# Three seven-product units for one batch of a sigmoid-attention and ReGLU kernel: batch 1's last four f chunks as a third unit, two chunks of batch 0 moved into batch 2

## The chip, the cores and the metric

The kernel runs on one core of a Trainium2 chip. The metric is device time of one execution in microseconds (us), median over runs. A core has engines that run side by side, each its own instruction stream in program order: TensorE (PE: matrix products, with its weight loads shown as PEld), VectorE (DVE: arithmetic element by element), ScalarE (ACT: functions such as sigmoid, copies), GpSimd (POOL: here above all the engine that issues loads) and SyncE (SP: here stores and transposing transfers). PE writes its results into eight banks of PSUM; DVE and ACT read them from there, and a bank can be written again only when its readers are through. Engines wait for one another by semaphores.

## The reference

```python
def _attn_ref(q, k, v):                      # 8 batches, 12 heads, 448 tokens, 64 per head
    scale = 1.0 / np.sqrt(q.shape[-1])
    scores = scale * np.matmul(q, k.transpose(0, 1, 3, 2)) - np.log(S)
    attn = 1.0 / (1.0 + np.exp(-scores))
    return np.matmul(attn, v)

def _moe_ref(x, w_gate, w_val, w_out):       # 3584 x 768, 768 x 1536 (twice), 1536 x 768
    gate = np.maximum(x @ w_gate, 0.0)
    val = x @ w_val
    return gate * val @ w_out
```

The attention's output, with heads side by side, is the x of the second part. Input and output are float32; the kernel multiplies in float16 and sums in float32.

## The kernel before

**Attention.** Heads go in groups of four, so a batch has three groups (g = 0, 1, 2). Tokens of a group go in seven chunks of 64 keys. `qk_unit` makes one chunk's scores: four matmuls into two banks (L239), then two sigmoids on ACT (L187), one for each bank. `pv_group` multiplies a whole group's probabilities with v: 28 matmuls into two banks (L257) and two evacuations on DVE (L184) into `xT`, the transposed x that the second part reads. The 21 chunks of a batch are cut into *bursts* (`cuts`), with the pv of one group within a burst (`pv_at`; that of a batch's last group lies in the next batch's first burst). Between two bursts PE does other work while ACT catches up on sigmoids.

**Keys and queries** must be transposed. For batch 0 and batch 1 PE does it (`pe_transposes`, L204, and a copy by DVE); from batch 2 on `dma_transposes(b, g)` does: two DVE copies into a buffer `rel` (L222; two such buffers) and a transposing transfer on SP's queue (L226) from `rel` to `qkT`.

**The second part.** f counts 12 chunks of 128 of the 1536 hidden columns. Simple form, `gv`: six matmuls for the gate and six for the value of one f chunk (L322), a relu (ACT, L334, or DVE, L336) and a multiplication on DVE (L343), result in `hT`. Batch 0's are computed in halves of 256 and 192 tokens (`push_first`), as filling in batch 1 (`ffn_mix`; `mix` says how many after which burst). All later work is done with seven products in place of eight, on sums of operand blocks:

- `gv_split` ("s", L688): one batch, four f chunks. Seven products of 12 matmuls on half of the tokens (L708), six copies out of PSUM (two of them on DVE, L719, four on ACT), six additions (L723) and four multiplications with relu (L729) on DVE. It needs sums of weight blocks (`early_sum_steps`, three sums and `gate_sums` for two chunks each) and of token blocks (`split_sums`).
- `gv_pair` ("w"): the same for two batches and two f chunks.
- `down_pair` ("y", L448): the last matmul for two tiles of 128 tokens, seven products of six matmuls (L385), on sums of `wo` (`weight_sums(0)` to `(3)`, 128x2304 each, L376) and of `hT` (`token_sum_steps`, 128x768 each). Where a burst lies amid it (`amid`, "inner burst"), the order of the seven products depends on whether the unit is in `SUMS_LATE`: if so, y11's product comes second, in a bank `a` taken at the beginning, and five products lie ahead of the inner burst; otherwise four, and y11's bank is taken behind it.

**Order.** Nothing is scheduled by a planner: each engine's order is the order in which this program writes its instructions. `for b in range(1, B)` goes through the batches; for each burst it writes the burst, then a filler with `jobs` (work of other engines written amid the filler, by `beside`) and `ahead` (written ahead of it). Batch 1's fillers are halves of batch 0; batch 2's come from `push_group(0)`: chunk 8 of batch 1, unit s0 (chunks 0 to 3), chunk 9, unit s4, chunks 10 and 11. Batch 3's fillers are the down units y of batches 0 and 1. PSUM banks are taken in turn from a ring (`free`); `later` changes the ring's order.

**Loads** are issued by POOL; a load waits until the one eight places before it has landed. `hold` puts a tiny POOL copy in the queue that waits for a transpose to land, so that later loads do not run beside it. Batch 1's k and q lie in the pool `early`, which also holds twelve `PT` buffers whose space the weight sums of s0 and s4 take over; `open_late` closes `early` and opens `late` with the sums of `wo` (`T`), `odd` and token-block sums (`X`).

Of the kernel before, what the change touches and what calls it, by code (L numbers as in the profile page):

```python
# [18 lines left out]
def kernel(  # L19
# [10 lines left out]
    nc = tc.nc  # L30
# [28 lines left out]
    gsbp = ctx.enter_context(tc.tile_pool(name="gsbp", bufs=6))  # L59
    first_sbuf = ExitStack()  # L60
# [34 lines left out]
    def tiles_of(b):  # L95
        if b not in in_tiles:
            pool = early if b == 1 else inp
            in_tiles[b] = tuple(
                p.tile([P, NPAIR, NCH * D], FP16, tag=t, name=t)
                for p, t in ((pool, "k16"), (pool, "q16"), (vinp, "v16"))  # L100
            )
        return in_tiles[b]
# [54 lines left out]
    load_gv(6, 9)  # L157
    load_v(1)
    load(1, 2, 3, "kq")
    load_gv(9, 12)  # L160
# [57 lines left out]
    def dma_transposes(b, g):  # L218
# [9 lines left out]
        )  # L228

# [136 lines left out]
    def open_late():  # L366
# [5 lines left out]
        late["X"] = pool.tile([P, 3, HD, S], FP16, tag="X", name="X")  # L372
        late["sums"] = ctx.enter_context(tc.tile_pool(name="sums", bufs=2))

# [28 lines left out]
    SUMS_LATE = {(1, 0), (1, 1), (2, 0), (2, 1), (3, NPP)}  # L403
# [152 lines left out]
    def early_sum_steps(j, f):  # L556
        views = []
        for i in range(3 * j, 3 * j + 3):
            t = early.tile([P, 2, 512], FP16, tag=f"PT{i}", name="S")
            flat = t[:].rearrange("p a y -> p (a y)")[:, 0 : HD * 2 * P]  # L560
            views.append(flat.rearrange("p (x y) -> p x y", y=2 * P))
# [15 lines left out]
    def batch_blocks(g, ks):  # L577
        x1, x2 = xT_tiles[2 * g], xT_tiles[2 * g + 1]
        lo, hi = slice(*ks), slice(HD + ks[0], HD + ks[1])
        return [late["X"][:, i, lo] for i in range(3)] + [x1[:, lo], x1[:, hi], x2[:, lo], x2[:, hi]]  # L580
# [13 lines left out]
    def gv_pair(g, f, beside, first_copy):  # L594
        x1, x2 = xT_tiles[2 * g], xT_tiles[2 * g + 1]
        T1, T2, T4 = (late["X"][:, i] for i in range(3))
# [77 lines left out]
    def split_sums(b):  # L674
        tile_ = xTp.tile([P, NPAIR, S], FP16, tag="xT", name="X2")
# [165 lines left out]
    push_first(1, range(0, 4))  # L841
    for f0 in range(4, 12, 2):
        for half in range(2):
            for f in range(f0, f0 + 2):
                push_first(half, (f,), (half, f) not in ((0, 9), (1, 8)))
# [10 lines left out]
    def hold(b, g):  # L856
        nc.gpsimd.tensor_copy(gate[0:1, :], qkT_tiles[(b, g)][0:1, 0, 0:2])
# [4 lines left out]

    def late_loads():
        dma_transposes(2, 2)
        hold(2, 1)
        load_v(2)
        load(3, 0, NG, "kq")
        load_o()

# [5 lines left out]
    def push_group(g):  # L875
        tail = [("y", g, p) for p in range(NPP)]
        if g == 0:
            work.extend([("u", 1, 8), ("s", 1, 0), ("u", 1, 9), ("s", 1, 4), ("u", 1, 10), ("u", 1, 11)])
# [45 lines left out]
    for b in range(1, B):  # L924
        if b == 1:
            cuts, pv_at = (0, 3, 6, 9, 13, 17, 21), {3: (0, 2), 5: (1, 2)}
        else:
            cuts, pv_at = (0, 4, 7, 11, 14, 18, 21), {0: (-1, 2), 2: (0, 2), 4: (1, 2)}
# [8 lines left out]
        if b == 1:  # L937
            mix = (4, 3, 3, 3, 3, 4)
            hooks = {
                1: [(3, lambda: both(1, 1))],  # L940
                3: [(3, lambda: both(1, 2))],
                4: [(2, lambda: dma_transposes(2, 0)), (0, lambda: dma_transposes(2, 1))],
                5: [(4, late_loads)],
            }
            steps = itertools.chain.from_iterable(early_sum_steps(j, 2 * j) for j in range(4))
            given = ((0, 0, 1, 1, 1), (0, 1, 1, 1), (0, 1, 1, 1), (0, 1, 1, 0), (2, 0, 0, 0), (0, 1, 1, 1, 0))
# [16 lines left out]
        for m in range(count):  # L963
# [92 lines left out]
```

## Time and profile before

| | us |
|---|---|
| median of 3 runs | 388.73 (388.58 to 389.12) |
| the profiled execution, its own time | 389.02 |
| its span, first to last instruction | 387.2 |
| PE busy | 381.0 |
| DVE busy | 304.5 |
| ACT busy | 227.3 |
| POOL busy | 49.9 |
| batch 1, span 29.0 to 61.3: DVE busy / ACT busy | 21.67 / 24.43 of 32.30 |
| batch 2, span 61.3 to 95.8: DVE busy / ACT busy | 26.39 / 23.72 of 34.50 |
| mean granted clock of PE | 0.998 |

Times in a trace count from the span's start. A line of the timeline gives start, length, engine, source line, operation, result and operands, shapes and how many instructions were merged into it; in brackets idle time ahead of it and what ended it. Durations overlap at their ends, so what one more instruction costs is read from start to start. The waits list says for each engine, line and cause how long it waited in all, how often, and the longest. Windows give span, then busy time and instruction count for PE, PEld, DVE, ACT and POOL, then granted clock, DMA share and GB/s.

### The profile page before, as it was taken

What the parts mean: (1) busy time and instruction counts of PE and PEld (TensorE: products, weight loads), DVE (VectorE), ACT (ScalarE), POOL (GpSimd) and SP (SyncE); (2) the same over time, 40 slices, a digit from 0 to 9 for tenths busy, and PEclk for the clock granted to TensorE, in tenths of its full rate; (3) what the DMA queues carried; (4) which work ended last, traced back from release to release, by engine and by line L of the source; (5) the groups of instructions that cost most, each with busy time, mean ns of one, the idle gap of its engine ahead of it and who ended that gap; (6) DMA issues with size and microseconds to landing.
All of it is one profiled execution on the core that took longest, in us unless ns stands there. A gap on an engine that the chain in (4) does not pass through costs nothing.

```text
span 387.2 us, 8977 instructions
## 1 busy us (share of the span) xinstructions
PE 381.0 (98%) x3570; PEld 223.2 (58%) x3570; DVE 304.5 (79%) x609; ACT 227.3 (59%) x480; POOL 49.9 (13%) x73
## 2 busy tenths in 40 slices
PE   8999999999999999999999999999999999999995
PEld 6678776885555545555555554545455555555563
DVE  3455667769868999999868789999978788999563
ACT  5967887567777645555777764545477344333321
POOL 9543306100400003000300300000000000000000
PEclk9999999999999999999999999999999999999999
DMA  9999999999969303952599893222012220000335
GB/s 169 199 199 204 204 194 163 208 208 130 182 150 193 81 2 40 184 90 47 44 228 224 164 231 60 48 50 50 0 38 72 71 69 0 2 0 0 83 88 159
DMA packets 67421, 43.81 MB, mean 113 GB/s; under 512 B 35634, under 2 KB 64050, under 8 KB 67378
## 3 DMA queue, kind: packets, MB, share of 16 engines
q0 software_dynamic: 28960, 23.24, 39.3%
q1 hardware_dynamic: 37634, 19.24, 24.4%
q10 hardware_dynamic: 784, 0.75, 0.6%
q8 instruction: 28, 0.46, 0.5%
q14 instruction: 15, 0.12, 0.1%
HBM read 47.19 MB, written 11.01 MB: 150 GB/s over the span
## 4 chain that ended last, share of the span: by engine, by line
PE 97%; ACT 2%; DVE 0%; issue 0%
PE u L385 35%; PE g L385 16%; PE y L385 12%; PE qk_ps L239 10%; PE pv_ps L257 8%; PE g_ps L322 5%; PE v_ps L322 5%; PE u L708 2%; PE g L708 2%; ACT PT L187 2%; PE warm_ps L175 1%; PE trt L204 1%; ACT ysb L446 0%; DVE ysb L540 0%; DVE zeros L130 0%
## 5 line engine op out<-in xcount | busy, mean ns | idle before, releaser
L187 ACT ACTIVATE PT<-qk_ps 128x448 f16<-128x448 f32 (+3 forms) x318 | 150.9, 584 | 79.7 <-PE qk_ps L239 79.5
L385 PEld LDWEIGHTS <-S 128*128 128x128 f16 x576 | 56.4, 98 | 45.9
L624 DVE TENSOR_TENSOR gsb<-g,gsb 128x448 f32<-128x448 f32 x72 | 42.8, 624 | 8.0 <-PE g L385 7.7
L239 PE MATMUL qk_ps<-qkT 64*64 64x448 f16 (+2 forms) x756 | 47.5, 337 | 1.0 <-ACT ysb L446 0.6
L385 PEld LDWEIGHTS <-hT 128*128 128x128 f16 x318 | 29.5, 98 | 24.0 <-issue 6.1
L257 PE MATMUL pv_ps<-PT,v 64*64 64x448 f16 (+2 forms) x756 | 36.6, 329 | 0.0
L464 DVE SCALAR_TENSOR_TENSOR ysb<-y,ysb 128x384 f32<-128x384 f32 x33 | 18.4, 556 | 21.3 <-PE y L385 14.3
L184 DVE TENSOR_SCALAR xT<-pv_ps 128x448 f16<-128x448 f32 (+2 forms) x53 | 27.8, 567 | 8.2 <-PE pv_ps L257 7.1
L385 PEld LDWEIGHTS <-wg 128*128 128x128 f16 x216 | 20.1, 98 | 21.8 <-issue 4.3
L385 PEld LDWEIGHTS <-wv 128*128 128x128 f16 x216 | 21.1, 98 | 19.7
L446 ACT ACTIVATE ysb<-u 128x384 f32<-128x384 f32 x28 | 13.8, 491 | 30.6 <-PE u L385 26.5
L239 PEld LDWEIGHTS <-qkT 64*64 64x64 f16 x756 | 17.7, 106 | 21.3 <-issue 14.2
L385 PE MATMUL u<-wo,hT 128*128 128x384 f16 x156 | 29.8, 327 | 0.0
L111 POOL DMA_DIRECT2D k<-in_k_dram x14 | 10.9, 776 | 142.0 <-DVE rel L222 136.3
L257 PEld LDWEIGHTS <-v 64*64 64x64 f16 x756 | 21.4, 107 | 11.1 <-issue 0.5
L385 PE MATMUL u<-xT,wg 128*128 128x448 f16 x108 | 23.5, 354 | 0.0
L385 PE MATMUL u<-X,S 128*128 128x448 f16 x108 | 23.4, 352 | 0.0
L385 PE MATMUL g<-xT,wg 128*128 128x448 f16 x108 | 23.4, 352 | 0.0
L385 PE MATMUL u<-X,wv 128*128 128x448 f16 x108 | 23.4, 352 | 0.0
L385 PE MATMUL g<-X,S 128*128 128x448 f16 x108 | 23.4, 352 | 0.0
L385 PE MATMUL g<-xT,S 128*128 128x448 f16 x108 | 23.4, 352 | 0.0
L385 PE MATMUL u<-xT,wv 128*128 128x448 f16 x108 | 23.4, 352 | 0.0
(98 smaller groups left out, 563.1 us busy)
## 6 DMA issues: line engine op xcount, KB each, us to landing
out_dram<-ysb SPq DMA_DIRECT2D x50, 192.0 KB, 3.9
v<-in_v_dram POOLq DMA_DIRECT2D x8, 336.0 KB, 15.3
v<-in_v_dram POOLq DMA_DIRECT2D x16, 168.0 KB, 15.2
k<-in_k_dram POOLq DMA_DIRECT2D x4, 672.0 KB, 12.0
q<-in_q_dram POOLq DMA_DIRECT2D x4, 672.0 KB, 15.0
wo<-in_moe_w_out_dram POOLq DMA_DIRECT2D x2, 1152.0 KB, 19.2
k<-in_k_dram POOLq DMA_DIRECT2D x9, 224.0 KB, 12.1
q<-in_q_dram POOLq DMA_DIRECT2D x7, 224.0 KB, 12.4
```

Source lines behind the costliest of these rows:

```text
L111: nc.gpsimd.dma_start(t16[:, xs, cs], rows_of(src, b)[:, xs, cs])
L175: nc.tensor.matmul(ps[:, 0:n], zeros[:, 0:P], zeros[:, 0:n], start=True, stop=True)
L184: nc.vector.tensor_scalar(out=xT, in0=src, scalar1=XSCALE, scalar2=None, op0=AOP.mult)
L187: nc.scalar.activation(PT_ap, ps_ap, AF.Sigmoid, bias=sig_bias, scale=qk_scale)
L239: nc.tensor.matmul(out_of(hh)[o : o + 64, :], qkT[rows, c, cols], qkT[rows, NCH + c0 : NCH + c1, cols], start=True, stop=True, tile_positi ...
L257: nc.tensor.matmul(ps[hh][64 * r : 64 * r + 64, 0:qn], v16[rows, 2 * g + hh, c * D : (c + 1) * D], pieces[c][rows, hh, :], start=(c == 0), ...
L322: nc.tensor.matmul(ps[:, 0:qn], (wg, wv)[i][:, dc, f * P : (f + 1) * P], xT_tiles[b][:, dc, q0 : q0 + qn], start=(dc == 0), stop=(dc == ND ...
L385: nc.tensor.matmul(ps[:, 0:n], A[:, k_, :], W[:, k_, :], start=(first and k_ == 0), stop=(k_ == kn - 1), skip_group_check=True,)
L446: nc.scalar.activation(o, ps[:, 0:HM], AF.Copy, scale=OUT_SCALE)
L464: nc.vector.scalar_tensor_tensor(out=o, in0=ps[:, 0:HM], scalar=OUT_SCALE, in1=o, op0=AOP.mult, op1=AOP.add)
L624: nc.vector.tensor_tensor(out=gs[u][i][:], in0=ps[u][:, 0:S], in1=gs[u][i][:], op=AOP.add)
L708: nc.tensor.matmul(ps[j // 2][:, j % 2 * SQ : (j % 2 + 1) * SQ], sets[j][i][:, k_, :], W[:, k_, :], start=(first and j % 2 == 0 and k_ == ...
```

## The change

- `push_group(0)`: batch 2's fillers become chunk 10 of batch 0, s0, chunk 11 of batch 0, s4 and a new unit s8 (batch 1's chunks 8 to 11). The 21 chunks of batch 2 are cut into five bursts (4, 3, 5, 4, 5) in place of six.
- Batch 1's mixes have 16 halves in place of 20 (3, 2, 3, 2, 3, 3). Six halves have their relu on DVE (before, two of those pushed there).
- s8's weight sums are computed in batch 2 in space of the output buffers `ysb` (`output_views`): one step beside the first filler, five beside chunk 11, two beside s4. `gate_sums` goes out of batch 3.
- `weight_sums(0)` and the first two token sums of (0,0) lie beside s8, `weight_sums(1)` ahead of batch 3's first down unit, the other two token sums and `weight_sums(2)`, `(3)` beside it. (0,0) is in `SUMS_LATE`.
- Transposes: (2,0) in batch 1's fifth mix, (2,1) and (2,2) beside batch 2's first two fillers, (3,0) and (3,1) beside s4, (3,2) beside s8.
- Loads: v of batch 1 earlier, wg and wv of chunks 6 to 8 around k/q (1,2), chunk 9 after batch 1's first burst, chunks 10 and 11, k/q (2,1), (2,2) and v2 behind a hold on the `rel` of (2,0); k/q of batch 3, `wo` and v3 behind a hold on the transposes of (2,1), in batch 2.
- Batch 1's k and q lie in a new pool `mid`, whose space `X2` (token sums of the s units) and `X` (those of the w units) take over.

The diff, without its context lines:

```diff
@@ -59,0 +60 @@
+    mid = ctx.enter_context(tc.tile_pool(name="mid", bufs=1))
@@ -97 +98 @@
-            pool = early if b == 1 else inp
+            pool = mid if b == 1 else inp
@@ -157 +157,0 @@
-    load_gv(6, 9)
@@ -158,0 +159 @@
+    load_gv(6, 9, (0,))
@@ -160 +161 @@
-    load_gv(9, 12)
+    load_gv(6, 9, (1,))
@@ -228,0 +230 @@
+        return rel
@@ -372 +373,0 @@
-        late["X"] = pool.tile([P, 3, HD, S], FP16, tag="X", name="X")
@@ -374,0 +376,4 @@
+    def open_X():
+        k16, q16 = (mid.tile([P, NPAIR, S], FP16, tag=t, name="X") for t in ("k16", "q16"))
+        late["X"] = [k16[:, 0:HD], k16[:, HD:NDC], q16[:, 0:HD]]
+
@@ -403 +408 @@
-    SUMS_LATE = {(1, 0), (1, 1), (2, 0), (2, 1), (3, NPP)}
+    SUMS_LATE = {(0, 0), (1, 0), (1, 1), (2, 0), (2, 1), (3, NPP)}
@@ -556,2 +561 @@
-    def early_sum_steps(j, f):
-        views = []
+    def early_views(j):
@@ -561 +565,10 @@
-            views.append(flat.rearrange("p (x y) -> p x y", y=2 * P))
+            yield flat.rearrange("p (x y) -> p x y", y=2 * P)
+
+    def output_views():
+        for _ in range(3):
+            t = ysbp.tile([P, 2, HD, 2 * P], FP16, tag="ysb", name="S")
+            yield t[:, 0]
+            yield t[:, 1]
+
+    def early_sum_steps(f, views):
+        views = list(itertools.islice(views, 3))
@@ -580 +593 @@
-        return [late["X"][:, i, lo] for i in range(3)] + [x1[:, lo], x1[:, hi], x2[:, lo], x2[:, hi]]
+        return [late["X"][i][:, lo] for i in range(3)] + [x1[:, lo], x1[:, hi], x2[:, lo], x2[:, hi]]
@@ -596 +609 @@
-        T1, T2, T4 = (late["X"][:, i] for i in range(3))
+        T1, T2, T4 = late["X"]
@@ -675 +688 @@
-        tile_ = xTp.tile([P, NPAIR, S], FP16, tag="xT", name="X2")
+        tile_ = mid.tile([P, NPAIR, S], FP16, tag="k16", name="X2")
@@ -841,2 +854,4 @@
-    push_first(1, range(0, 4))
-    for f0 in range(4, 12, 2):
+    push_first(1, range(0, 3))
+    push_first(1, (3,), False)
+    by_vector = {(1, 3), (0, 5), (0, 6), (1, 6), (1, 7), (0, 9)}
+    for f0 in range(4, 10, 2):
@@ -845 +860 @@
-                push_first(half, (f,), (half, f) not in ((0, 9), (1, 8)))
+                push_first(half, (f,), (half, f) not in by_vector)
@@ -856,2 +871,2 @@
-    def hold(b, g):
-        nc.gpsimd.tensor_copy(gate[0:1, :], qkT_tiles[(b, g)][0:1, 0, 0:2])
+    def hold(t):
+        nc.gpsimd.tensor_copy(gate[0:1, :], t[0:1, 0, 0:2])
@@ -863,3 +878,5 @@
-    def late_loads():
-        dma_transposes(2, 2)
-        hold(2, 1)
+    def loads_behind_first():
+        hold(dma_transposes(2, 0))
+        load_gv(10, 12)
+        load(2, 1, 2, "kq")
+        load(2, 2, 3, "kq")
@@ -866,0 +884,3 @@
+
+    def late_loads():
+        hold(qkT_tiles[(2, 1)])
@@ -868,0 +889 @@
+        load_v(3)
@@ -878 +899 @@
-            work.extend([("u", 1, 8), ("s", 1, 0), ("u", 1, 9), ("s", 1, 4), ("u", 1, 10), ("u", 1, 11)])
+            work.extend([("u", 0, 10), ("s", 1, 0), ("u", 0, 11), ("s", 1, 4), ("s", 1, 8)])
@@ -928 +949,2 @@
-            cuts, pv_at = (0, 4, 7, 11, 14, 18, 21), {0: (-1, 2), 2: (0, 2), 4: (1, 2)}
+            cuts = (0, 4, 7, 12, 16, 21) if b == 2 else (0, 4, 7, 11, 14, 18, 21)
+            pv_at = {0: (-1, 2), 2: (0, 2), 4: (1, 2)}
@@ -938 +960 @@
-            mix = (4, 3, 3, 3, 3, 4)
+            mix = (3, 2, 3, 2, 3, 3)
@@ -940,4 +962,3 @@
-                1: [(3, lambda: both(1, 1))],
-                3: [(3, lambda: both(1, 2))],
-                4: [(2, lambda: dma_transposes(2, 0)), (0, lambda: dma_transposes(2, 1))],
-                5: [(4, late_loads)],
+                1: [(2, lambda: both(1, 1))],
+                3: [(2, lambda: both(1, 2))],
+                4: [(3, loads_behind_first)],
@@ -945,2 +966,2 @@
-            steps = itertools.chain.from_iterable(early_sum_steps(j, 2 * j) for j in range(4))
-            given = ((0, 0, 1, 1, 1), (0, 1, 1, 1), (0, 1, 1, 1), (0, 1, 1, 0), (2, 0, 0, 0), (0, 1, 1, 1, 0))
+            steps = itertools.chain.from_iterable(early_sum_steps(2 * j, early_views(j)) for j in range(4))
+            given = ((0, 0, 1, 1), (0, 1, 1), (1, 1, 1, 1), (0, 1, 1), (1, 1, 0, 1), (1, 1, 1, 0))
@@ -968,3 +989 @@
-            if b == 2 and m == 3:
-                jobs += [lambda: dma_transposes(3, 0), lambda: dma_transposes(3, 1)]
-            elif b == 3 and m == count - 1:
+            if b == 3 and m == count - 1:
@@ -978,0 +998 @@
+                    load_gv(9, 10)
@@ -980,3 +1000 @@
-                    load(2, 1, 2, "kq")
-                    load(2, 2, 3, "kq")
-            elif m == (2 if b == 4 else 0) and b + 1 < B:
+            elif b > 2 and m == (2 if b == 4 else 0) and b + 1 < B:
@@ -986,9 +1004,17 @@
-            if b == 2 and m == 0:
-                ahead.append(lambda: split_sums(1))
-            elif b == 2 and m == 4:
-                open_late()
-                first_sums = token_sum_steps(0, 0)
-                ahead += [*first_sums[:2], lambda: weight_sums(0)]
-            elif b == 2 and m == 5:
-                ahead += [lambda: weight_sums(1), lambda: dma_transposes(3, 2)]
-                jobs += first_sums[2:]
+            if b == 2:
+                if m == 0:
+                    views = output_views()
+                    steps = itertools.chain.from_iterable(early_sum_steps(f, views) for f in (8, 10))
+                    ahead.append(lambda: split_sums(1))
+                    jobs += [lambda: dma_transposes(2, 1), lambda: next(steps)()]
+                elif m == 1:
+                    jobs += [lambda: dma_transposes(2, 2), late_loads]
+                elif m == 2:
+                    jobs += [lambda: next(steps)()] * 5
+                elif m == 3:
+                    jobs += [lambda: next(steps)()] * 2
+                    jobs += [lambda: dma_transposes(3, 0), lambda: dma_transposes(3, 1)]
+                else:
+                    open_late()
+                    first_sums = token_sum_steps(0, 0)
+                    jobs += [lambda: weight_sums(0), *first_sums[:2], lambda: dma_transposes(3, 2)]
@@ -996,5 +1022,4 @@
-                jobs.append(lambda: (weight_sums(2), weight_sums(3)))
-            elif b == 3:
-                jobs.append(lambda: gate_sums(6 + 2 * m, 8 + 2 * m))
-                if m == 1:
-                    jobs.append(lambda: keep_odd(0))
+                ahead.append(lambda: weight_sums(1))
+                jobs += [*first_sums[2:], lambda: weight_sums(2), lambda: weight_sums(3)]
+            elif b == 3 and m == 1:
+                jobs.append(lambda: keep_odd(0))
@@ -1002,0 +1028,2 @@
+                    if b == 3:
+                        open_X()
```

More of the change, by code (lines that the diff above doesn't have):

```diff
@@ L861, in both @@
         pe_transposes(b, g, 1)
+    def loads_behind_first():
[3 more added lines that the diff above has]
+        load(2, 2, 3, "kq")
+        load_v(2)
     def late_loads():
-        dma_transposes(2, 2)
-        hold(2, 1)
-        load_v(2)
+        hold(qkT_tiles[(2, 1)])
         load(3, 0, NG, "kq")
         load_o()
+        load_v(3)
     work = deque()
```

## The prediction

> **What bounds the kernel now.** I read the page first (busy shares, slices, chain), then the waits of PE, the windows by stage, and the timelines of PE, ACT and DVE over batch 2, where the edit lies.
>
> ```profile
> PE 381.0 (98%) x3570; PEld 223.2 (58%) x3570; DVE 304.5 (79%) x609; ACT 227.3 (59%) x480; POOL 49.9 (13%) x73
> DVE  3455667769868999999868789999978788999563
> PE 97%; ACT 2%; DVE 0%; issue 0%
> PE qk_ps L239 <- ACT ysb L446: 0.6, 1, 0.6
> 29.00:61.30 32.30, 32.30 (x444) 26.26 (x443) 21.67 (x53) 24.43 (x60) 8.54 (x12) 1.00 1.22 197
> 61.30:95.80 34.50, 34.50 (x387) 24.68 (x387) 26.39 (x49) 23.72 (x54) 6.69 (x10) 1.00 1.16 184
> ```
>
> PE is the whole chain and waits for almost nothing; the last two lines (span, then busy time and instructions of PE, weight loads, DVE, ACT, POOL; granted clock; DMA) say that batch 1 and batch 2 are PE without a gap at full clock. So PE time is worth its full length, but only while the other engines keep up. In batch 2 DVE has 26.39 us of 34.50 busy: 8.1 us of room. That room is what this change draws on. The timeline of PE (batch 1's end, then batch 2):
>
> ```profile
> 58.56 0.82 PE L322 MATMUL v_ps<-xT,wv 128*128 128x256 f16 x6
> 59.21 0.66 PE L322 MATMUL g_ps<-xT,wg 128*128 128x192 f16 x6
> 63.49 1.31 PE L322 MATMUL g_ps<-xT,wg 128*128 128x448 f16 x6
> 65.87 0.76 PE L239 MATMUL qk_ps<-qkT 64*64 64x448 f16 x12
> 66.56 1.32 PE L708 MATMUL u<-xT,wg 128*128 128x224 f16 x12
> 74.72 0.57 PE L239 MATMUL qk_ps<-qkT 64*64 64x448 f16 x8
> ```
>
> ACT and DVE over the same stage (start, duration of the group, line, operation, shapes, count, idle time before it):
>
> ```profile
> 75.14 3.60 ACT L187 ACTIVATE PT<-qk_ps 128x448 f16<-128x448 f32 x8 [4.33 <-PE qk_ps L239]
> 78.56 0.62 ACT L334 ACTIVATE gate_sb<-g_ps 128x448 f32<-128x448 f32 x1
> ```
>
> ```profile
> 80.78 1.20 DVE L719 COPY gsb<-u 128x448 f32<-128x448 f32 x2 [0.68 <-PE u L708]
> 81.89 0.38 DVE L222 COPY rel<-k 128x896 f16<-128x896 f16 x1
> 84.23 1.20 DVE L723 TENSOR_TENSOR gsb<-g,gsb 128x448 f32<-128x448 f32 x2 [1.04 <-PE g L708]
> 91.15 0.55 DVE L434 TENSOR_TENSOR S<-hT 128x768 f16<-128x768 f16 x1
> 97.82 1.15 DVE L184 TENSOR_SCALAR xT<-pv_ps 128x448 f16<-128x448 f32 x2
> 99.19 0.56 DVE L441 TENSOR_SCALAR ysb<-u 128x384 f32<-128x384 f32 x1 [0.21 <-PE u L385]
> 99.66 1.35 DVE L376 TENSOR_TENSOR wo<-wo 128x2304 f16<-128x2304 f16 x1
> 100.93 1.35 DVE L376 TENSOR_TENSOR T<-wo,T 128x2304 f16<-128x2304 f16 x1
> 102.20 0.55 DVE L464 SCALAR_TENSOR_TENSOR ysb<-y,ysb 128x384 f32<-128x384 f32 x1
> ```
>
> Prices, start to start: PE: a whole f chunk 2.38 (63.49 to 65.87), a three-chunk burst 0.69, a split unit 8.16 (66.56 to 74.72), a burst of four chunks with its pv 2.20. ACT: a sigmoid 0.427 (8 in 75.14 to 78.56), the first one 0.42 after its burst. DVE: unit operations 0.555 (80.78 to 81.89 for two), rel copies 0.31, weight sums 1.27, 128x768 sums 0.50 on average (91.15 to 92.21, 96.89 to 97.82), a pv evacuation 0.535. DVE starts a unit's additions at once when they are ready (it idled 2.25 and 1.04 ahead of them); inside a unit it needs 1.11 per pair against PE's 1.15 per product, so lateness there is not made up.
>
> **The change part by part.** PE alone first. Removed: four whole chunks of batch 1, 4 x 2.38 = 9.52; four halves of batch 0 in batch 1, 2 x 0.99 (192 columns, 47.58 to 48.57) + 2 x 1.31 (256 columns, 57.90 to 59.21) = 4.60. Added: unit s8, 8.16; two whole chunks, 4.76. Bursts in batch 2: three of 2.20 and three of 0.69 become 2.20, 0.69, 2.39, 0.88, 2.39 (a chunk 0.19, from 0.69 against 0.88, a bare four-chunk burst): 8.55 for 8.67. Sum: 8.16 + 4.76 - 9.52 - 4.60 - 0.12 = **-1.32 us**. Batch 2 begins 4.60 earlier, at 56.7, its third burst (call it t0) at 70.1, batch 3 at t0+24.36 = 94.5 (before 95.79).
>
> DVE does not get less. Into batch 2 come s8's 12 operations for four chunks' multiplications, 8 sum steps (two of them were in batch 3 before), and rel (3,2) moves ahead of s8's additions. From t0 on I lay ACT's and DVE's queues out in the order of the program:
>
> - t0: the burst has five chunks, ten sigmoids, and chunk f11's relu stands behind them: 0.42 + 10 x 0.427 = 4.7, 0.62 long, so its multiplication starts at 5.4 on DVE (before, with eight sigmoids, 3.84 after the burst). Behind it on DVE stand all the following: five sum steps, two copies of s4, two sums, four rel copies, ten operations of s4, pv evacuation, two copies of s8, weight sum 0, two token sums, two rel copies, ten operations of s8, batch 3's pv evacuation, weight sum 1, the first output copy, two token sums, weight sums 2 and 3, and the addition of y11.
> - Their work: multiplication 0.55, 11 sums x 0.50 = 5.5, 6 rel copies 1.86, 24 unit operations 13.3, 4 evacuations 2.14, 4 weight sums 5.08, output copy 0.47, addition 0.55: 29.5. DVE has one gap of about 0.2 (s8's first copy, which needs PE). So the addition ends at 5.4 + 29.7 = t0+35.1.
> - Who waits for it: (0,0) is now in SUMS_LATE, so y11 has its bank early, and the inner burst's third chunk takes that bank. PE without waits gets there at 24.36 + 2.20 + 5 products x 0.985 (98.00 to 100.94 for three) + two chunks 0.45 = t0+31.95. **PE loses 35.1 + 0.05 - 31.95 = 3.2 us**, in steps: the fourth burst's last bank (f11's multiplication) 0.4, s4's third product (the copy behind five sums) 0.5, s8's first bank (pv evacuation behind s4's operations) 0.7, and the rest at the inner burst. Even with all the earlier ones gone, the last one stays: evacuation done 3.2 after batch 3's start, then 1.27 + 0.47 + 1.0 + 2.54 + 0.55 = 9.0, against PE's 7.6: **1.4, alone more than the gain**. Before, the two weight sums stood there too (99.66 to 102.20), but weight sum 1 had begun at 94.0, and y11's bank was asked for only behind the inner burst, so no burst waited for its reader.
> - Bounds of this term: DVE's work is all of it rows, so only overlap can change it: below, 1.4; above 3.9 (0.55 for each sum, as the longest rows, and 0.57 for a unit operation).
>
> Transfers. Transposes of (3,0) are now asked for by DVE: the rel copy of (3,2) needs the buffer that they read (rel has two), at t0 + 22.1 = 92.2. Behind it stand s8's additions, hence the whole chain. Before, (3,0) was issued at 82.6 behind the loads of wo and v3 and landed at 93.3, 1.1 after v3's last load (92.2). Now the hold waits for (2,1) instead of letting v2 go at 60.2; k3 to v3 took 23.6 us behind v2, so from about 67.7 they end at 91.3 to 93.3 and the transposes at 92.4 to 94.4. Wait: from 0 (landed before) to 2.2; I take **1.6**, by the row of the same transfer.
>
> The rest. Four more relus on DVE and eight fewer on ACT in batch 1: 0.35 each (the row of a 192-column operation), hidden, as DVE idles 10.6 us there (32.30 - 21.67); bounds 0 to 0.5. Loads moved on POOL's queue (v1 ahead of wg 6 to 9; wv 6 to 9 behind k/q of (1,2); wg/wv 9 to 12 later): needed at 44 at the earliest by the third burst's mix, landing at 43.5 by the pace of before: 0, bound 1. The two holds' waits stand on POOL, where only loads queue behind them. Store of (0,0) in two pieces on SP, behind which no transpose waits for 5 us: 0. Gate sums gone from batch 3: 0, since PE is the bound there and DVE idled 1.14 and 0.42 at 103 to 105.
>
> Sum: -1.32 + 3.2 + 1.6 = +3.5. The profiled execution took 389.02 (span 387.2 and 1.8 around it), 0.29 over the median; on the median's scale 388.73 + 3.5 = **392.2 us**.
>
> **The rivals.**
> 1. Faster: DVE's late work is covered and the chip keeps PE's sum, 388.73 - 1.32 = 387.4. Decided at one place: the addition of y11 must end by t0+32, so DVE must be through batch 3's evacuation and three weight sums 3.2 us sooner than its rows add up to. For it: 98% PE, DVE had 8.1 us of room in batch 2. Against: all of that room is spoken for above. 0.08.
> 2. Transposes (3,0) land before DVE asks: 388.73 - 1.32 + 3.2 = 390.6. For: alone, a transpose took 3.9 (the shortest landing in its row). Against: 10.6 for this very transfer. 0.22.
> 3. Transposes (2,0) late as well. They are issued at about 48.4, 8.3 before batch 2 needs them, but now POOL's loads start right behind. Landings with nothing beside: 3.9, median 5.0; the longest, beside k and q loads, 11.9. By the first two no wait, by the last 60.3, a wait of 3.6, so 392.2 + 3.6 = 395.8; in between, 394. Before they had the queues almost alone (53.6 to 58.2). 0.18. [...]
> 4. Half of it: the early waits are absorbed and only the last one is paid, no transfer late: -1.32 + 1.4, within 0.2% of before, 388.8. 0.06.
>
> **How the numbers follow.** My forecast, 392.2, has 0.46, its own range 391.2 to 393.8. Rivals 2 and 3 also end slower. 0.2% is 0.8 us, about what a measurement of this kernel can tell from no change. Faster: rival 1, 0.08. Same: rival 4, 0.06. Slower: 0.46 + 0.22 + 0.18 = 0.86. The range leaves out rivals 1 and 4 and the far end of 3: 389.9 to 395.3.
>
> **What would show it.** PE should begin batch 2 near 56.7 and the third burst near 70.1; if batch 2 begins late with a wait for the transposes of (2,0), rival 3. PE's waits, nearly none before, should now name DVE: the multiplication of f11 (L343 before), a unit copy, a pv evacuation, and the longest the addition of y11 at the inner burst. DVE should be without idle time from 75 to 106 but for one wait of a rel copy on a transpose near 92; if that wait is missing, rival 2. DVE's busy share in batch 2 should be near 95%, against 76%. The prediction is wrong if DVE shows idle time ahead of s4's or s8's additions, or if PE goes from batch 3's first product to the inner burst without a wait.

## The result and the profile after

The changed kernel takes **400.18 us** (median of four runs, 398.31 to 400.27), against 388.93 for the kernel before measured with it: a ratio of **1.0277, 95% interval 1.0245 to 1.0309**. The forecast was 392.2 with a range of 389.9 to 395.3. Slower was right; the loss is three times the forecast one. (One run each of two kernels below, the filled wait and the sums alone, fell into a slower state of the chip and is left out of their numbers.)

The page of the changed kernel (busy times; then PE, granted clock and DMA in 40 slices of 9.96 us; then the chain by engine):

```profile
PE 383.6 (96%) x3582; PEld 226.2 (57%) x3582; DVE 313.2 (79%) x627; ACT 225.5 (57%) x473; POOL 51.4 (13%) x76
PE   8999989997799999999999999999999999999995
PEclk9999999999699999999999999999999999999999
DMA  9999999999982910693299898022203330000235
PE 83%; DMA 9%; DVE 3%; POOL 2%; ACT 1%; issue 1%; POOLq 0%; DVEq 0%
```

DMA, which had no share of the chain before, now has 9% of it, and PE has two slices at 7 from 90 to 110 us, one of them with the clock at 6 tenths. Nearly all of it lies between 57 and 118 us; behind that the two kernels run in parallel. PE's waits (engine, line, what it waited for: total, times, longest):

```profile
PE u L721 <- DVE gsb L736: 5.3, 1, 5.3
PE qk_ps L241 <- DMA qkT<-rel: 1.9, 1, 1.9
PE qk_ps L241 <- DVE ysb L469: 0.9, 1, 0.9
PE v_ps L324 <- DMA wv<-in_moe_w_val_dram: 0.4, 1, 0.4
PE u L721 <- DVE gsb L732: 0.3, 1, 0.3
```

PE's timeline at those places (batch 2 begins at 58.98, t0 is 72.41, batch 3 begins at 104.76):

```profile
58.98 0.57 PE L241 MATMUL qk_ps<-qkT 64*64 64x448 f16 x8 [1.89 <-DMA qkT<-rel]
72.41 0.57 PE L241 MATMUL qk_ps<-qkT 64*64 64x448 f16 x8
77.43 1.41 PE L241 MATMUL qk_ps<-qkT 64*64 64x448 f16 x16
81.58 1.31 PE L721 MATMUL u<-X,S 128*128 128x224 f16 x12 [0.34 <-DVE gsb L732]
102.43 2.40 PE L721 MATMUL u<-X,wv 128*128 128x224 f16 x12 [5.26 <-DVE gsb L736]
104.76 0.96 PE L241 MATMUL qk_ps<-qkT 64*64 64x448 f16 x8
105.50 2.70 PE L259 MATMUL pv_ps<-PT,v 64*64 64x448 f16 x28
115.13 0.38 PE L241 MATMUL qk_ps<-qkT 64*64 64x448 f16 x3 [0.88 <-DVE ysb L469]
```

The wait of 5.26 names DVE, but DVE was waiting itself. Its timeline there:

```profile
93.84 0.56 DVE L381 TENSOR_TENSOR S<-S,hT 128x768 f16<-128x768 f16 x1
100.08 0.39 DVE L223 COPY rel<-k 128x896 f16<-128x896 f16 x1 [5.68 <-DMA qkT<-rel]
100.69 1.15 DVE L736 TENSOR_TENSOR gsb<-g,gsb 128x448 f32<-128x448 f32 x2
113.26 1.35 DVE L381 TENSOR_TENSOR T<-wo,T 128x2304 f16<-128x2304 f16 x1
114.53 1.01 DVE L469 SCALAR_TENSOR_TENSOR ysb<-y,ysb 128x384 f32<-128x384 f32 x2
```

The copy into `rel` for (3,2) waits until the transposes of (3,0) have landed, at 100.06; s8's additions stand behind it, and PE's last product of s8 behind those. And the product that follows is slow: 2.40 where 1.31 is usual, the pv burst 2.70 where 1.49 is. Windows of the same execution (span, busy times, granted clock, DMA):

```profile
95.80:101.20 5.40, 1.36 (x15) 1.21 (x13) 1.11 (x3) 0.00 (x0) 0.43 (x1) 0.99 1.32 176
101.40:107.10 5.70, 4.67 (x40) 2.76 (x43) 4.79 (x9) 1.71 (x4) 2.36 (x4) 0.50 1.02 156
107.10:109.00 1.90, 1.90 (x27) 0.86 (x20) 0.75 (x2) 0.64 (x3) 0.45 (x1) 0.77 1.26 207
```

Some 4 us into its standstill, at 101.13, PE's clock fell to 0.50, and it stayed there until 107.96 (the 0.77 of the last window has 0.86 us of half clock in it).

The balance, from the two profiled executions, up to the burst behind the inner one (105.73 before, 117.50 after):

| | us | from |
|---|---|---|
| PE's own work | -1.31 | what is left of the sum, not measured by itself; -1.32 by the rows |
| transposes of (2,0) late 1.89, a wait for wv 0.4 near 20 (some other executions have it too) | +2.29 | batch 2 begins at 58.98, not 56.69 |
| DVE's and ACT's short waits from t0 to s8 | +1.50 | 0.25 + 0.45 + 0.50 + 0.30 at the burst of t0, the next one, s4, the fifth |
| transposes of (3,0) late | +5.40 | s8 14.65 instead of 8.16, less the slow product |
| half clock | +2.64 | product 1.09, pv burst 3.76 instead of 2.21 |
| inner burst | +1.24 | 113.50 to 115.44, 1.94 instead of 0.70 |
| sum | +11.76 | 117.50 - 105.73 = 11.77 |

Later 0.62 comes back, since the profiled execution of before has a wait of 0.6 of its own near 210 that none of the others has.

### The profile page after: what moved, and what is told of

It reads as the page before. It is cut to its first block, busy times and chain, and to the rows that moved or that the text cites. A ratio compares the mean times of both kernels' runs of the same rounds, so it can differ in the third digit from the quotient of the medians.

```text
span 398.5 us, 9012 instructions
## 1 busy us (share of the span) xinstructions
PE 383.6 (96%) x3582; PEld 226.2 (57%) x3582; DVE 313.2 (79%) x627; ACT 225.5 (57%) x473; POOL 51.4 (13%) x76
## 4 chain that ended last, share of the span: by engine, by line
PE 83%; DMA 9%; DVE 3%; POOL 2%; ACT 1%; issue 1%; POOLq 0%; DVEq 0%
PE u L390 33%; PE g L390 15%; PE y L390 11%; PE qk_ps L241 8%; PE pv_ps L259 7%; DMA qkT<-rel 7%; DMA wv<-in_moe_w_val_dram 3%; PE g_ps L324 3%; PE v_ps L324 2%; PE u L721 2%; ACT PT L188 1%; PE g L721 1%; POOL q L112 1%; PE trt L205 1%; DVE S L381 0%
## 5 line engine op out<-in xcount | busy, mean ns | idle before, releaser
L241 PE MATMUL qk_ps<-qkT 64*64 64x448 f16 (+2 forms) x756 | 48.6, 338 | 3.5 <-DMA qkT<-rel 1.9
L259 PE MATMUL pv_ps<-PT,v 64*64 64x448 f16 (+2 forms) x756 | 37.8, 336 | 0.0
L241 PEld LDWEIGHTS <-qkT 64*64 64x64 f16 x756 | 18.4, 106 | 25.0 <-issue 16.4
```

The lines of the kernel that those rows point to most:

```text
L241: nc.tensor.matmul(out_of(hh)[o : o + 64, :], qkT[rows, c, cols], qkT[rows, NCH + c0 : NCH + c1, cols], start=True, stop=True, tile_positi ...
L259: nc.tensor.matmul(ps[hh][64 * r : 64 * r + 64, 0:qn], v16[rows, 2 * g + hh, c * D : (c + 1) * D], pieces[c][rows, hh, :], start=(c == 0), ...
```

## Experiments

**1. Are the transfers late because they share the queues?** Three kernels, each the changed one with one edit. First, v3 behind the transposes of (3,0):

```diff
         load(3, 0, NG, "kq")
         load_o()
-        load_v(3)
...
+                hold(qkT_tiles[(3, 0)])
+                load_v(3)
```

> The changed kernel (400.2) with the loads of v3 moved behind the landing of the transposes (3,0). Theory (the transposes (3,0) share the queues packet for packet and land only when the loads ahead are through): they land 0.5 us behind the second half of wo (94.98 or a little sooner), at 95 to 96 instead of 100.06; the rel copy of (3,2) waits about 1 instead of 5.7, PE's wait at s8's last product falls from 5.26 to about 1, the clock stays up: 6 to 7 us faster, 393.5. Rival (the transposes take 16 us for a reason of their own, such as the order of issue on SP): (3,0) still lands near 100, no change.

Measured: 394.70 (392.75 to 394.99), ratio 1.0143 (1.0116 to 1.0171). (3,0) landed at 96.97, wo's second half at about 95. PE's waits of that execution:

```profile
PE qk_ps L241 <- DMA qkT<-rel: 2.6, 1, 2.6
PE u L721 <- DVE gsb L736: 1.8, 1, 1.8
```

5.26 became 1.81, the product behind it took 1.31 again, and 5.5 us came back, less than the 6 to 7 expected. The transposes land once the loads ahead of them are through, as the theory said, but 1.9 behind wo and not 0.5; and in this execution batch 2's start waited 2.6 instead of 1.9.

Second, a buffer of its own for `rel` of (3,2), so that DVE need not wait:

```diff
-        rel = relp.tile([P, TW, P], FP16, tag="rel", name="rel")
+        if (b, g) == (3, 2):
+            rel = late["rel"]
+        else:
+            rel = relp.tile([P, TW, P], FP16, tag="rel", name="rel")
...
-        late["odd"] = pool.tile([P, NFC, P], FP16, tag="odd", name="odd")
+        late["rel"] = pool.tile([P, TW, P], FP16, tag="odd", name="odd")
+        late["odd"] = late["rel"][:, 0:NFC, :]
```

> The changed kernel (400.2) with a buffer of its own for the rel copies of (3,2), so that they need not wait for the transposes of (3,0). Loads and transposes stay. Theory (the transposes of (3,0) are late by themselves): DVE's wait of 5.7 and PE's of 5.26 go, but batch 3's first burst, at 98.4 by then, waits for the same transposes until 100.1: 1.7 of wait there, the clock stays up, the inner burst waits 1.3: 5.7 faster, 394.5. Rival (only the shared buffer was at fault): all of 5.3 + 2.6 comes back, 392.3.

Measured: 397.71 (395.58 to 399.74), ratio 1.0220 (1.0167 to 1.0272). The wait moved as expected, but another came. PE's timeline, batch 3's beginning and 22 us later, and DVE's ahead of the second:

```profile
100.10 0.57 PE L244 MATMUL qk_ps<-qkT 64*64 64x448 f16 x8 [1.06 <-DMA qkT<-rel]
122.43 1.69 PE L394 MATMUL y<-wo,hT 128*128 128x384 f16 x6 [3.09 <-DVE ysb L473]
121.35 0.56 DVE L421 COPY odd<-hT 128x1536 f16<-128x1536 f16 x1 [6.12 <-DMA qkT<-odd]
```

DVE was free, and batch 3's first burst waited for (3,0) all the same, at 100.05. The freed buffer also let batch 4's loads start 5 us sooner (95.73 for 100.77), beside (3,1) and (3,2), which landed at 110.18 and 121.33 instead of 101.63 and 107.97. That was paid at 122, since the buffer is not quite its own: it takes the space of `odd`, and DVE's copy into `odd` waited 6.12 until the transposes of (3,2) had read it. So neither theory had the time (394.5 and 392.3), though the place of the first wait was right.

Third, POOL's first hold on the landing of (2,0), with nothing loading beside it:

```diff
-        hold(dma_transposes(2, 0))
+        dma_transposes(2, 0)
+        hold(qkT_tiles[(2, 0)])
```

> The changed kernel (400.2) with POOL's first hold on the landing of the transposes of (2,0) instead of their rel copy, so that no load runs beside them. Theory (they took 10.2 us, 48.78 to 58.94, because loads took every other packet): they land in 4 to 5 us, near 53, batch 2 begins at 57.0 without its wait of 1.89, loads land 2 us later at first and not later from the hold on (2,1) on: 1.9 to 4 us faster, 396.2 to 398.3. Rival (late for another reason): still 58.9, no change.

Measured: 399.37 (398.34 to 399.98), ratio 1.0271 (1.0250 to 1.0293). The DMA view of this run from 48 to 53 us (queue, packets, MB, share; then landing), and of the changed kernel from 50 to 58 us (total, then queue 0 with the loads and queue 1 with the transposes):

```profile
q1 hardware_dynamic: 1824, 0.46, 48.6%
qkT<-rel SPq DMA_TRANSPOSE x1, 4.1
```

```profile
DMA packets 3131, 1.16 MB, mean 146 GB/s; under 512 B 1759, under 2 KB 3130, under 8 KB 3130
q0 software_dynamic: 1387, 0.70, 77.8%
q1 hardware_dynamic: 1743, 0.45, 53.7%
```

Alone the transposes of one group took 4.1 us here; beside loads (2,0) took 10.2 in the changed kernel (48.78 to 58.94). From 50 to 58 us there 1743 packets of the transposes went beside 1387 of the loads, which is near the "every other packet" of the expectation; in what order one engine took them is not shown. The packets of a transpose hold 256 bytes (0.45 MB in 1743), those of the loads about 500 (0.70 MB in 1387). Together the two had 146 GB/s, where loads alone had 184 and 189 (55 to 57 and 57 to 59 us of this run) and transposes alone 223 (68 to 70 of the changed kernel); the transposes got 0.45 of the 1.16 MB. Batch 2 began at 56.54 without a wait, 2.4 sooner, but 1.1 of that was lost at a load of wv, which the hold had made later, and 1.3 at s8, with the longer wait:

```profile
PE v_ps L324 <- DMA wv<-in_moe_w_val_dram: 1.1, 1, 1.1
PE u L721 <- DVE gsb L736: 6.6, 1, 6.6
```

since (2,1) now went beside v2 and landed at 71.18 (before the edit 69.78), the hold on it let k3 go at 71.91 (70.50), and (3,0) landed at 100.21 as if nothing had been done. The order of the transfers, not this one transfer, sets when (3,0) lands.

**2. Is the slow stretch the clock?** The wait is filled with work:

```diff
         plus(2, p)
+        for _ in range(4 if f == 8 else 0):
+            product(c, 3, T1)
         product(c, 6, B22, False)
```

> The changed kernel (400.2) with one thing added: in unit s8 the second product is computed four more times into its own bank, ahead of the sixth product. Nothing else moves; it fills the 5.26 us in which PE waits for an addition with 4 x 1.15 = 4.6 us of PE work. Theory (the wait lowers PE's granted clock, and the product and pv burst behind it run at half pace: 2.33 and 3.76 us where 1.25 and 2.21 are usual): they are back at 1.25 and 2.21, so up to 2.6 us faster, less up to 0.9 that comes back at the inner burst as DVE is not earlier: 397.6 to 398.5. Rival (they are slow because of DMA or DVE traffic beside them): the same slow product and burst, 400.2.

Measured: 399.14 (398.80 to 399.20, three runs), ratio 1.0266 (1.0249 to 1.0283). PE's timeline at s8's end and the window of batch 2's beginning in the same execution:

```profile
98.25 4.76 PE L721 MATMUL g<-X,S 128*128 128x224 f16 x48
104.00 1.31 PE L721 MATMUL u<-X,wv 128*128 128x224 f16 x12
105.24 0.57 PE L241 MATMUL qk_ps<-qkT 64*64 64x448 f16 x8
105.65 1.49 PE L259 MATMUL pv_ps<-PT,v 64*64 64x448 f16 x28
```

```profile
59.70:63.20 3.50, 3.46 (x44) 1.73 (x44) 0.29 (x1) 1.85 (x4) 0.00 (x0) 0.58 1.27 204
```

With PE busy, product and pv are back at 1.31 and 1.49 and the burst at 2.21: the 2.64 us are the clock. The time fell by 1.0 only, because in this execution the transposes of (2,0) took 1.1 longer, and behind PE's wait of 3.02 there the clock halved from 60.23 to 63.65 (the window's 0.58 is a mean): the same thing at another place.

**3. How much is transfers, how much DVE?** Two sets of edits, alone and together. Loads and transposes in another order:

```diff
+                    load(2, 0, 1, "kq")
                     load_gv(9, 10)
-                    load(2, 0, 1, "kq")
+                    load_gv(10, 12)
...
-                3: [(2, lambda: both(1, 2))],
-                4: [(3, loads_behind_first)],
+                3: [(2, lambda: both(1, 2)), (0, loads_behind_first)],
...
-        hold(dma_transposes(2, 0))
-        load_gv(10, 12)
+        dma_transposes(2, 0)
+        hold(qkT_tiles[(2, 0)])
...
-        load_v(3)
...
+                hold(qkT_tiles[(3, 0)])
+                load_v(3)
```

> The changed kernel (400.2) with only loads and transposes in another order: k/q (2,0) ahead of weight chunk 9, chunks 10 and 11 right behind, transposes (2,0) at the end of batch 1's fourth mix, POOL's first hold on their landing, v3 behind the landing of (3,0). No instruction of DVE's sums is moved. Theory (nearly all that was lost is late transfers and the clock behind the long wait): batch 2 starts at 56.6 without a wait, wv is there in time, (3,0) lands at 91 to 93, PE waits 0 to 1 at s8, no slow product, and what is left is DVE's short waits (0.2 + 0.45 + 0.35 + 0.3) and 1 to 1.4 at the inner burst: 390 to 391. Rival (the transfers cannot be had in time, since the queues have no room before batch 3): (3,0) lands near 97 as with v3 later alone, 394.

DVE's sums in another order:

```diff
-                    jobs += [lambda: next(steps)()] * 5
+                    ahead += [lambda: next(steps)()] * 4
+                    jobs += [lambda: next(steps)()]
...
-                jobs += [*first_sums[2:], lambda: weight_sums(2), lambda: weight_sums(3)]
+                jobs += first_sums[2:]
+                after_add.extend([lambda: weight_sums(2), lambda: weight_sums(3)])
...
             plus(y1[:, lo], a)
+            while after_add:
+                after_add.popleft()()
```

> The changed kernel (400.2) with only DVE's sums in another order: four of the five sum steps ahead of chunk 11's multiplication (DVE idles 2.28 there), weight sums 2 and 3 behind the addition of y11. Theory (DVE's own order costs little as long as (3,0) is late): the wait of 0.34 in s4 goes and comes back as a longer wait at s8, since (3,0) lands when it did; the 0.88 at the inner burst goes: 399.3. Rival (DVE's queue is the cause, as the prediction's term of 3.2 had it): 397 or less.

Both:

> The edits of both together. Theory: loads in time, then DVE's order counts in full: the waits in s4 (0.35) and at the inner burst (1 to 1.4) go, those behind f11's relu (0.45) and at the fourth and fifth burst (0.2 and 0.3) stay, some 0.3 at T4: 1.3 to 1.7 under the run with loads alone, 388.5 to 389.3, the same as before the change. Rival (PE's sum of -1.32 is not there in the first place): 390 or more with no wait left.

In the last two the fourth step ahead of chunk 11, a gate sum, replaces the weights that this chunk's value product reads, so chunk 11 of batch 0 is computed from the sum and not from its weights, and these two kernels do not compute the reference; the amount of work is the same, but the product waits 1.19 for DVE.

| | us | ratio | PE's waits that count |
|---|---|---|---|
| loads | 392.76 (391.46 to 394.57) | 1.0114 (1.0090 to 1.0137) | s8 2.9, inner burst 1.1, s4 0.3 |
| sums | 398.80 (397.71 to 400.57, three runs) | 1.0270 (1.0245 to 1.0294) | s8 3.0, (2,0) 2.4, value product 1.2 |
| both | 391.50 (390.39 to 394.07) | 1.0079 (1.0055 to 1.0103) | s8 2.6, value product 1.2 |

The loads alone bring 7.4, the sums alone 1.4, and the sums on top of the loads 1.3, in spite of the 1.2 that the value product waits. With spreads of about 3 us in each kernel that does not show whether DVE's order is worth less while (3,0) is late, as was expected. Both sets together missed the 388.5 to 389.3 expected, and the loads alone fell short of 390 to 391. PE's and DVE's waits of the run with the loads alone:

```profile
PE u L721 <- DVE gsb L736: 2.9, 1, 2.9
DVE rel L223 <- DMA qkT<-rel: 3.3, 1, 3.3
```

(3,0) landed at 94.94, behind the second half of wo at 93.11, and DVE still stood before it.

**4. What is left when the copy of (3,2) goes?** On the loads' edits, the copy behind the addition of y11:

```diff
-                    jobs += [lambda: weight_sums(0), *first_sums[:2], lambda: dma_transposes(3, 2)]
+                    jobs += [lambda: weight_sums(0), *first_sums[:2]]
...
+                after_add.append(lambda: dma_transposes(3, 2))
```

> The run with loads in another order (392.8), with the rel copies of (3,2) out of s8, behind the addition of y11 in batch 3; the sums stay in the changed kernel's order. Theory: PE's 2.9 at s8 goes, batch 3 begins near 95.6, and DVE's own queue is all that is left: 0.34 in s4 and 1.4 at the inner burst, 390.2, and 1.5 to 1.9 above the run with the sums moved as well. Rival (the inner burst's wait was only the tail of the late transposes): no wait there, 388.9, and no difference to the run with the sums moved.

and with the sums as well (three steps ahead of chunk 11, which then reads its own weights again, and the copy behind weight sum 3):

```diff
-                    ahead += [lambda: next(steps)()] * 4
-                    jobs += [lambda: next(steps)()]
+                    ahead += [lambda: next(steps)()] * 3
+                    jobs += [lambda: next(steps)()] * 2
...
-                after_add.extend([lambda: weight_sums(2), lambda: weight_sums(3)])
+                after_add.extend([lambda: weight_sums(2), lambda: weight_sums(3), lambda: dma_transposes(3, 2)])
```

> The kernel with both loads and sums in another order, with two more edits: three sum steps instead of four ahead of chunk 11 (the fourth made the value product wait 1.2 us), and the rel copies of (3,2) out of s8, behind weight sum 3 in batch 3. Theory (what is left is (3,0) landing at 95 behind the second half of wo, and DVE standing in front of s8's additions until then): no wait at s8, batch 3 begins at 95.1 to 95.6 just as (3,0) is there, no wait at the inner burst, 0.3 at T4: 388.2 to 389.0, the same as before the change. Rival (each wait that is taken out comes back elsewhere, the chip has no room for the third unit here): 390 or more.

Measured: 391.91 (1.0089, 1.0076 to 1.0102) and 391.95 (1.0099, 1.0074 to 1.0124). Batch 3 began at 95.57 and 95.11, as expected, the second 0.68 ahead of the kernel before. PE's waits of the second:

```profile
PE qk_ps L241 <- DMA qkT<-rel: 1.7, 1, 1.7
PE y L391 <- DVE ysb L470: 0.9, 1, 0.9
```

The copy of (3,2) frees the buffer that batch 4's keys are loaded into. Put behind, it held back those loads (104.47 for 95.96 in the kernel before), and batch 4's first burst waited 1.67 for its transposes. Both expectations missed that reader.

**5. A version without these waits.** The copy back beside s8, but in a buffer of its own (the space of `odd` again), v3 behind (3,1), the first output copy of (0,0) on ACT:

```diff
-                hold(qkT_tiles[(3, 0)])
+                hold(qkT_tiles[(3, 1)])
...
-            down_pair(g, i, beside, prepare, not work, scaled_act if alone else scaled, amid)
+            down_pair(g, i, beside, prepare, not work, scaled_act if alone or (g, i) == (0, 0) else scaled, amid)
```

> The last version with all edits (391.2 to 392, of which 0.85 at T4 and 1.67 at batch 4's first burst are there because the rel copies of (3,2) come late and k and q of batch 4 load behind them), with the rel copies of (3,2) back beside s8 but in a buffer of their own, v3 behind the landing of (3,1), and the first output copy of (0,0) on ACT. Theory (PE's 1.3 us are there once transfers and DVE are in time): batch 3 begins at 95.1 as it did, T4 waits 0 to 0.3, no wait at batch 4: 388.3 to 388.9, the same as before the change and the best with three units. Rival (every place for the work of (3,2) costs, since queues and DVE are full): 390 or more.

Measured: **388.65** (388.22 to 388.98), ratio 0.9998 (0.9990 to 1.0007): the same as before, 11.5 us under the changed kernel with the same number of PE's instructions. A last edit on it, the next unit's first two token sums behind the evacuations of (0,0):

```diff
-                for step in steps[:2]:
+                for step in steps[: 0 if (g, p) == (0, 0) else 2]:
                     step()
...
             (scaled if amid else scaled_act)(y2[:, lo], b)
+            if (g, p) == (0, 0):
+                for step in steps[:2]:
+                    step()
```

> The last version (388.65, the same as before the change), with the first two token sums of the next down unit behind the two evacuations of the third product of (0,0) instead of ahead of them, so that the bank that the next pv takes comes free 1 us sooner. Theory (what is left of the third unit's loss is DVE in batch 3: that pv burst takes 6.69 to the inner burst, where 6.21 is usual): 0.3 to 0.5 less, 388.2 to 388.4, at the edge of what can be told from before the change. Rival (the sums are then late for the next unit's first product that needs them): no change, 388.6.

Measured: **388.03** (387.45 to 388.26) against 388.43, ratio **0.9986 (0.9977 to 0.9995)**: 0.14% under the kernel before. The interval leaves out 1, but the difference is smaller than the 0.2% that the prediction called about what can be told from no change. The page's busy line and PE's waits, then three of batch 2's bursts and what follows them:

```profile
PE 380.3 (98%) x3582; PEld 225.1 (58%) x3582; DVE 312.7 (81%) x626; ACT 225.6 (58%) x474; POOL 51.6 (13%) x77
PE warm_ps L176 <- DVE zeros L131: 1.2, 1, 1.2
PE qk_ps L244 <- ACT PT L188: 0.3, 1, 0.3
70.03 0.57 PE L244 MATMUL qk_ps<-qkT 64*64 64x448 f16 x8
72.67 1.31 PE L327 MATMUL g_ps<-xT,wg 128*128 128x448 f16 x6
75.04 1.41 PE L244 MATMUL qk_ps<-qkT 64*64 64x448 f16 x16
76.38 1.32 PE L731 MATMUL u<-xT,wg 128*128 128x224 f16 x12
84.53 0.57 PE L244 MATMUL qk_ps<-qkT 64*64 64x448 f16 x8
87.18 1.32 PE L731 MATMUL u<-xT,wg 128*128 128x224 f16 x12
```

The list has no wait that the kernel before lacked, and yet PE's 1.32 us are not had. From batch 1's first burst to the one behind batch 3's inner burst this version takes 76.38 us (28.89 to 105.27), the kernel before 76.73: 0.35 less. The rest is in the three bursts shown. The two with five chunks take 2.64 and 2.65, not 2.39, and the bare one of four 1.34, not 0.88: 0.97 more than was added up. In this trace the fifth chunk's last bank is written from 72.36 and 86.86 on, each time 0.05 behind the end of a sigmoid, and the four-chunk burst's last bank from 76.07, 0.06 behind f11's multiplication. The list does not show these waits, as the records of PE's matmuls overlap. Whether other cuts of the bursts would save them was not tried.

**6. Had the kernel before room in its queues?** One edit on the kernel before:

```diff
-        hold(2, 1)
+        hold(2, 2)
```

> The kernel before (388.6) with one change: the hold ahead of v2, batch 3's k and q, wo and v3 waits for the transposes of (2,2) instead of (2,1), so that these loads start 2.9 us later (63.05 for 60.16). Theory (the queues are full up to batch 3 in the kernel before too, and (3,0) lands as soon as the loads are through): (3,0) lands 2 to 3 us later, at 95.5 to 96.2 instead of 93.3, DVE's rel copy of (3,2) waits for it and f11's multiplication behind it, and PE waits 0.5 to 2 us ahead of or at batch 3's first burst: 389.1 to 390.6. Rival (there is room in the queues of the kernel before; only the changed kernel is short): 388.6, no wait.

Measured: 389.09 (388.38 to 391.14), ratio 1.0020 (1.0003 to 1.0036). (3,0) landed at 95.56, 2.3 later, with the loads (94.73). In the profiled execution (388.78) DVE's copy of (3,2) waited 0.2 for it and PE not at all, as batch 3 began at 95.83:

```profile
95.58 0.39 DVE L222 COPY rel<-k 128x896 f16<-128x896 f16 x1 [0.18 <-DMA qkT<-rel]
```

So the landing follows the loads here too, but the kernel before had slack: its transposes land at 93.28, 2.0 ahead of DVE's copy (95.28) and 2.5 ahead of batch 3 (95.79). The spread to 391.14, where the kernel before ends at 389.61, suggests that PE is reached in some executions and not in others. The median lies at the lower edge of what was expected; PE's wait that was expected is not in the profile.

## Why the prediction was wrong in size

- **PE's sum, -1.32.** The products came as the rows said: 13.43 us from batch 2's first burst to t0, and in the last version batch 2 begins 4.58 sooner, counted from batch 1's first burst (4.60). The bursts did not. The 2.39 for five chunks was not a row but 2.20 and one chunk more, and it took 2.64 and 2.69; the 0.88 for a bare burst of four was not one either (the row was 1.02, 49.98 to 51.00), and it took 1.33, of which 0.4 was forecast in DVE's term. The balance's -1.31 does not show this, as it is what is left over and has the bursts under the short waits.
- **DVE's queue, 3.2.** The mechanism and its places were right; the size was 2.2: 0.45 at the fourth burst (0.4 forecast), 0.5 at s4 (0.5), hardly anything at s8's first bank (0.7) and 1.24 at the inner burst. The other 0.55 of the short waits are the two bursts of five chunks. (The upper bound of 3.9 adds up to 4.1 by its own rows.) DVE runs a pair of unit operations in 1.06 to 1.07 when it is behind (100.69 to 101.76), not 1.11, so it catches up by 0.08 for each of PE's 1.15. That "lateness there is not made up" was wrong.
- **Transposes of (3,0), 1.6 of 0 to 2.2.** This is the step that failed. DVE asked at 94.4 and the landing was at 100.06: 5.68, and 5.40 of it reached PE. Of the 8.3 us that the forecast lacks, 3.8 are here, 2.64 are the clock behind this wait and 2.29 batch 2's start. The forecast moved the stretch "k3 to v3 took 23.6 us" as one block behind a hold that would open at 67.7. The hold opened at 69.9, because (2,1) was issued at 65.2, behind batch 2's late start; k3 then landed 7.1 us after its issue, as (2,2) ran until 72.04; and wo's second half took 8.0 us instead of 5.7, with (3,0), issued at 83.66, beside all of it (in the kernel before, issued at 82.64, beside the last 4.1 us of it). The duration of a queue of loads is not a constant that can be moved: it contains the transposes that share it.
- **Transposes of (2,0), kept as rival 3 at 0.18.** It happened, with 10.2 us of landing out of the 3.9 to 11.9 that were named: 1.89 us at batch 2's start, as a part of 3.6. The rows that the prediction had, 3.9 with nothing beside and 11.9 beside loads, deserved more than that chance: both transposes came late beside loads, with 10.2 for (2,0) and 16.4 for (3,0).
- **The clock, not in the sum.** 2.64 us. The waits were added up as if a wait cost only itself.
- The view that was not read: the kernel before's DMA slices,

```profile
DMA  9999999999969303952599893222012220000335
```

eleven slices in a row at 9, up to 106 us. (The prediction's two window lines have it too, as DMA shares of 1.22 and 1.16.) PE at 98% hid that the queues were nearly as full as PE up to batch 3, with the 2 us of room of experiment 6. The change starts batch 2 4.6 us sooner and must bring the same bytes and transposes by then; the prediction costed each transfer by itself, and never the queues as an engine with a sum of its own.

What would have shown it was written down: the wait of a rel copy near 92 (seen, 5.68 at 94.4), the wait for (2,0) (seen), the longest PE wait at the inner burst (wrong: at s8), DVE near 95% busy in batch 2 (wrong: 74%, with the standstill in it).

## What to carry to other kernels

When an edit makes one engine's stage shorter, add up every resource of that stage again, the DMA queues too: a stage at 98% PE with DMA slices at 9 has two bounds, and work brought forward finds the transfers where they were. A burst with more chunks than PSUM has room for is priced with the engine that empties the banks, not by PE's rows (here 2.64 and 2.65 us for five chunks, 2.39 by the rows). Put transposes with small packets where nothing else is loading (one group's took 4.1 us alone and 10.2 beside loads), and look at what stands behind a wait on an in-order engine: here one copy into a shared buffer passed a late transfer on to ten operations and PE. A wait of PE costs more than its length if the clock drops behind it (here 2.64 more for one of 5.26).

## What the runs showed of the hardware

- After some of PE's waits the granted clock halved. In the changed kernel PE stood still from 97.16 to 102.43, and the clock was 0.50 from 101.13 to 107.96; at the end of its wait of 1.89, from 57.09 to 58.98, and up to 65 it was 1.00. In the experiments half clock came with a wait of 2.4 at batch 2's start (the sums alone, 0.50 from 60 to 63 us), of 3.02 there (the filled wait, 0.50 from 61 to 63), of 2.6 at s8 (both sets, 0.58 from 97 to 99 and 0.57 from 99 to 101) and of 6.6 at s8 (the hold on the landing, 0.50 from 99 to 105). After a wait of 3.09 in the run with a buffer for `rel` two products took 1.69 and 2.13, where 1.15 is usual. Full clock, 1.00 in the windows over and behind the wait, came with waits of 2.6 and 1.81 (v3 later), 2.9 at batch 2's start (the buffer for `rel`), 2.9 at s8 (the loads alone) and 3.0 at s8 (the sums alone). So from 2.4 to 3.0 the length of a wait did not decide alone, and what else did is not shown; of these waits those up to 1.89 kept full clock, and those of 5.26 and 6.6 did not.
- Beside loads a group's transposes were slow: from 50 to 58 us of the changed kernel 1743 transpose packets of 256 bytes went beside 1387 load packets of about 500, and the transposes took 10.2 us, against 4.1 with nothing beside them in the run with the hold on the landing. Beside the larger packets of wo and v3 (1286 transpose packets against 1499 from 86 to 98 us, 175 GB/s together) the transposes got 0.33 MB in 12 us. (3,0) landed 1.1 us behind the last load that was issued ahead of it in the kernel before (93.28 behind 92.16) and 0.5 in the changed kernel (100.06 behind 99.58).
